# Moving the last two sums of W2's Strassen blocks to other places in VectorE's queue

## The chip, the cores and the metric

The kernel runs on one core of a Trainium2 chip. The metric is device time in microseconds (us) of one execution. The engines are named as in the profile: PE is the tensor engine, PEld its weight loads, DVE is VectorE, ACT is ScalarE, POOL is GpSimd and SP is SyncE. In these traces each engine works through its own queue in order.

## The reference

The program is a linear attention followed by a two-layer network. Cut to what matters:

```python
q_s = softmax(q, axis=-1)                        # 8 batches, 8 heads, 576 rows, 64 columns
k_s = softmax(k, axis=2)
kv  = einsum('bhsd,bhse->bhde', k_s, v)
x   = einsum('bhsd,bhde->bhse', q_s, kv)         # regrouped to 4608 x 512
h   = x @ w_in                                   # 512 x 2048
g   = h * sigmoid(h)
out = g @ w_out                                  # 2048 x 512
```

## The kernel before

The 4608 rows go through in nine chunks of 512 (the first two are of 576 and 448). In chunk t (t from 2 on) the tensor engine interleaves two kinds of work: the 16 **up-projections** of chunk t (`mm1`, numbered 0 to 15 in the order in which they run) and the output product of chunk t-1. That output product is done by Strassen's scheme of seven **products** in the order 1, 5, 6, 2, 7, 4, 3, each in two halves. Most of their operands are sums of blocks: `s_op` makes S1 to S4 from the activations in every chunk, and `t_op` makes T1 to T4 from W2 once in the program. Product 7 reads T3, and product 4 reads T4. All of these sums run on VectorE.

```python
def silu(t, fb, i, o, w):
    ...
    nc.scalar.activation(out=s, in_=i, func=ACT.Tanh, scale=OS)               # L244
    nc.vector.scalar_tensor_tensor(                                           # L245: "GT"
        out=o, in0=s, scalar=1.0, in1=i, op0=ALU.add, op1=ALU.mult)           # in1 is in PSUM

def mm1(t, fb):                      # one up-projection
    bank = hb[0] % hb[1]             # 3 banks from chunk 2 on
    hb[0] += 1
    mm1_mm(t, fb, bank, range(NC))   # L272
    mm1_silu(t, fb, bank)

def t_op(i, eng, f0=0, f1=HF):       # L345; all operands in SBUF
    o, in0, in1 = {
        1: (T1, B12, B11),
        2: (T2, B22, T1),
        3: (T3, B22, B12),           # T3 is written over B12 itself
        4: (T4, B21, T2),
    }[i]
    f = slice(f0, f1)
    eng.tensor_tensor(out=o[:, f], in0=in0[:, f], in1=in1[:, f], op=ALU.subtract)
```

There are three banks, so up-projection k can start only when VectorE has written GT of up-projection k-3. A VectorE that falls behind therefore stops the tensor engine three up-projections later.

The program is a list of units, one per up-projection or half product. `plan(u, f)` emits work just before unit u. In chunk 2, up-projections 0 to 12 are at units 0, 1, 3, 5, 7, 9, 11, 13, 15, 17, 19, 21 and 22. After the first product of the chunk (unit 2), units 21 and 22 are the only place where two come without a product between them. Product 7 begins at unit 18 and product 4 at unit 23. The units touched in chunk 2 (`begin[2]`):

```python
# sums of the activations, for every chunk t
plan(begin[t] + 2, lambda t=t: (s_op(t - 1, 1)))
plan(begin[t] + 4, lambda t=t: (s_op(t - 1, 2)))
plan(begin[t] + 10, lambda t=t: (s_op(t - 1, 3)))
plan(begin[t] + 15, lambda t=t: (s_op(t - 1, 4)))
# ... cut ...
plan(begin[2] + 7, lambda: t_op(4, nc.vector, 0, 4))
plan(begin[2] + 8, lambda: t_op(4, nc.vector, 4, 8))
plan(begin[2] + 12, lambda: t_op(3, nc.vector, 0, 4))
plan(begin[2] + 13, lambda: t_op(3, nc.vector, 4, 8))
# ... cut: the attention of the next batch b = t + 1, in each chunk t (units 5, 7 and 9, 12) ...
for i, x in enumerate((4, 6)):
    pl(x, lambda i=i, b=b: exp_q(b, i))
    pl(x + 1, lambda i=i, b=b: (qsum(b, i), qnorm(b, i, nc.gpsimd)))   # L142, L146 on VectorE; L151 on GpSimd
for i, x in enumerate((9, 12)):
    pl(x, lambda i=i, b=b: (exp_k(b, i), vcast(b, i, nc.gpsimd)))      # L89 on GpSimd
# (the loads of batch b + 1, which stand in these loops too, are cut)
```

The two `qnorm` instructions are called the norms below, and the two `vcast` instructions the casts.

The softmax here doesn't subtract the row's maximum and nothing guards it: scores larger than these inputs give would overflow.

Of the kernel before, what the change touches and what calls it, by code (L numbers as in the profile page):

```python
# [17 lines left out]
def kernel(  # L18
# [9 lines left out]
    nc = tc.nc  # L28
# [280 lines left out]
    def mm2_plain_out(t, ms):  # L309
        ow = mp.tile([128, 2, DM], FP32, name="ow", bufs=3)  # L310
        for i, m in enumerate(ms):
            if i == 0:
                nc.scalar.activation(out=ow[:, i], in_=PS[:, 2 + m], func=ACT.Copy, scale=OS)
            else:
                nc.vector.tensor_scalar_mul(out=ow[:, i], in0=PS[:, 2 + m], scalar1=OS)
            store(t, m * 128, ow[:, i])
# [20 lines left out]
    def t_op(i, eng, f0=0, f1=HF):  # L337
# [3 lines that stand above are left out]
            3: (T3, B22, B12),  # L341
# [4 lines that stand above are left out]
# [160 lines left out]
    def plan(u, f):  # L506
        at.setdefault(u, []).append(f)
# [7 lines left out]
    begin = {1: len(units)}  # L515
# [141 lines left out]
    for i, x in enumerate((25, 28)):  # L657
        plan(b1 + x, lambda i=i: xt(2, i))
    plan(b1 + 30, lambda: mm2_plain_out(0, (2, 3)))
    plan(begin[2] + 7, lambda: t_op(4, nc.vector, 0, 4))  # L660
    plan(begin[2] + 8, lambda: t_op(4, nc.vector, 4, 8))
    plan(begin[2] + 12, lambda: t_op(3, nc.vector, 0, 4))
    plan(begin[2] + 13, lambda: t_op(3, nc.vector, 4, 8))

    for t in range(2, NCH - 1):
        b = t + 1
# [58 lines left out]
```

## Time and profile before

| | before |
|---|---|
| median of the first three runs | 277.86 us (277.34 to 278.49) |
| the profiled execution | 277.1 us, span 275.3 us |
| chunk 2, first product to first product of chunk 3 | 31.04 us |
| chunk 3, measured likewise | 27.78 us |

The page's busy table says for each engine the busy time, the share of the span and the number of instructions:

```profile
PE 266.0 (97%) x2372; PEld 168.3 (61%) x2372; DVE 201.5 (73%) x291; ACT 158.3 (57%) x237; POOL 70.6 (26%) x62
```

The tensor engine bounds the kernel. The table of the tensor engine's waits says who waited for whom, the total in us, how often, and the longest:

```profile
PE PS L272 <- DVE GT L245: 2.4, 3, 1.2
```

Three waits, all in chunk 2, come to 2.4 us. The loss itself is better read from the tensor engine's timeline. Its columns are start, duration, engine and line, operation, operands, count, and in brackets the idle time before it and what ended it:

```profile
65.30 1.04 PE L361 MATMUL PS<-W,GT 128*128 128x256 f16 x8
...
76.22 1.02 PE L272 MATMUL PS<-XT,W 128*128 128x512 bf16 x4 [1.20 <-DVE GT L245]
...
79.08 1.02 PE L272 MATMUL PS<-XT,W 128*128 128x512 bf16 x4 [0.97 <-DVE GT L245]
...
81.17 1.02 PE L272 MATMUL PS<-XT,W 128*128 128x512 bf16 x4 [0.19 <-DVE GT L245]
82.14 1.19 PE L361 MATMUL PS<-W,S 128*128 128x256 f16 x8
83.33 1.02 PE L272 MATMUL PS<-XT,W 128*128 128x512 bf16 x4
...
96.34 1.04 PE L361 MATMUL PS<-W,GT 128*128 128x256 f16 x8
...
109.37 1.03 PE L272 MATMUL PS<-XT,W 128*128 128x512 bf16 x4
...
111.11 1.03 PE L272 MATMUL PS<-XT,W 128*128 128x512 bf16 x4
...
124.12 1.04 PE L361 MATMUL PS<-W,GT 128*128 128x256 f16 x8
```

The lines at 65.30, 96.34 and 124.12 us are the first half products of chunks 2, 3 and 4. Chunk 2 takes 31.04 us and chunk 3, with the same matmuls, 27.78 us. So chunk 2 loses 3.26 us, not 2.4. The rest hides where no idle time is recorded. In the undisturbed flow the record of one group overlaps the next by 0.17 us (65.30 + 1.04 = 66.34, and the next group starts at 66.17), so each of the three waits is recorded about 0.16 us too short: 0.5 us in all. The other 0.42 us is at product 7 (82.14), which shows 1.19 us instead of 1.04: the up-projection at 83.33 starts 2.16 us after the one at 81.17, where the undisturbed step in chunk 3 is 1.74 us (109.37 to 111.11). The Trainium skill ("Perfetto Trace Analysis", section "Identifying the Most-Contended Engine") warns that matmul busy time is a poor measure of how close a kernel is to roofline (its peak rate), because matmuls are pipelined. This trace agrees in so far as 0.9 of the 3.26 us does not appear as idle time.

Two timelines point to the cause. This is VectorE's, in chunk 2:

```profile
71.17 0.63 DVE L245 SCALAR_TENSOR_TENSOR GT<-sg,PS 128x512 f16<-128x512 f32 x1
71.71 2.35 DVE L345 TENSOR_TENSOR T<-W,T 128x1024 f16<-128x1024 f16 x1
73.98 1.34 DVE L142 TENSOR_REDUCE zq<-eq 128x18 f32<-128x1152 bf16 x1
...
75.54 0.63 DVE L245 SCALAR_TENSOR_TENSOR GT<-sg,PS 128x512 f16<-128x512 f32 x1
76.08 2.35 DVE L345 TENSOR_TENSOR T<-W,T 128x1024 f16<-128x1024 f16 x1
78.36 0.68 DVE L245 SCALAR_TENSOR_TENSOR GT<-sg,PS 128x512 f16<-128x512 f32 x1
78.95 1.56 DVE L335 TENSOR_TENSOR S<-GT 128x2048 f16<-128x2048 f16 x1
...
81.04 1.64 DVE L345 TENSOR_TENSOR W<-W 128x1024 f16<-128x1024 f16 x2
```

And this is GpSimd's:

```profile
71.40 2.12 POOL L151 TENSOR_TENSOR eq<-eq,rzq 128x1152 bf16<-128x1152 bf16 x1 [16.21 <-ACT sg L244]
75.77 2.12 POOL L151 TENSOR_TENSOR eq<-eq,rzq 128x1152 bf16<-128x1152 bf16 x1 [2.25 <-DVE rzq L146]
77.83 3.71 POOL L89 CAST vaug<-vt 128x1152 bf16<-128x1152 f32 x2
```

The two instructions of 2.35 us are T4's halves. Each starts 0.3 us after a norm and ends 0.54 us after the norm's end (73.52 and 74.06 for the first). The GT lines at 75.54 and 78.36 us end just when the tensor engine's waits end.

### The profile page before, as it was taken

To read this page: it belongs to the slowest core of one execution; us is meant where nothing else is said; L and a number is where in the kernel's file an instruction comes from. 1 tells how busy PE (TensorE), PEld (TensorE's weight loads), DVE (VectorE), ACT (ScalarE), POOL (GpSimd) and SP (SyncE) were. 2 spreads that over 40 slices of the span, in tenths; PEclk is the share of its full clock that TensorE was granted. 3 is DMA by queue.
4 is the path that set the end of the run, shared out by engine and by line. 5 is a ranking of instruction groups with operands and counts; after the bars stand their busy time and mean duration, and the time that the engine had idled before them with its cause. 6 is when DMAs were issued, how large, how long until landed. Compare 5 with 4: busy or idle time off the path is not lost.

```text
span 275.3 us, 5801 instructions
## 1 busy us (share of the span) xinstructions
PE 266.0 (97%) x2372; PEld 168.3 (61%) x2372; DVE 201.5 (73%) x291; ACT 158.3 (57%) x237; POOL 70.6 (26%) x62
## 2 busy tenths in 40 slices
PE   8999999999879999999999999999999999999993
PEld 3467654455645666656665666566656665666783
DVE  2867765969999399839984898489847673767643
ACT  5757937677833685467646764576455446444410
POOL 1744960900380019000900090009000000000003
PEclk9999999999999999999999999999999999999998
DMA  7999999599856386837693769342224003300444
GB/s 255 313 203 358 259 334 332 158 307 374 279 98 250 79 214 187 278 80 195 198 288 79 207 177 288 68 93 44 45 55 101 2 0 76 79 0 0 93 101 114
DMA packets 35498, 45.85 MB, mean 167 GB/s; under 512 B 16208, under 2 KB 20048, under 8 KB 35472
## 3 DMA queue, kind: packets, MB, share of 16 engines
q1 hardware_dynamic: 29568, 33.69, 43.6%
q0 software_dynamic: 5584, 11.54, 16.1%
q8 instruction: 18, 0.29, 0.5%
q10 hardware_dynamic: 320, 0.26, 0.3%
q14 instruction: 8, 0.07, 0.1%
HBM read 36.70 MB, written 9.44 MB: 168 GB/s over the span
## 4 chain that ended last, share of the span: by engine, by line
PE 85%; DVE 9%; ACT 2%; DMA 1%; POOL 1%; issue 1%; POOLq 0%
PE PS L272 38%; PE PS L361 34%; PE PS L301 5%; PE PS L252 4%; PE PS L222 2%; PE PS L183 2%; DVE zq L142 2%; DVE T L345 2%; DVE GT L245 2%; DVE S L335 1%; DMA qt<-in_q_dram 1%; DVE eq L151 1%; ACT eq L106 1%; ACT sg L244 1%; POOL t L120 0%
## 5 line engine op out<-in xcount | busy, mean ns | idle before, releaser
L245 DVE SCALAR_TENSOR_TENSOR GT<-sg,PS 128x512 f16<-128x512 f32 (+2 forms) x144 | 96.3, 678 | 53.3 <-ACT sg L244 52.9
L244 ACT ACTIVATE sg<-PS 128x512 f32<-128x512 f32 (+2 forms) x144 | 85.7, 598 | 83.7 <-PE PS L272 79.1
L272 PE MATMUL PS<-XT,W 128*128 128x512 bf16 (+1 forms) x512 | 126.5, 376 | 2.6 <-DVE GT L245 2.4
L272 PEld LDWEIGHTS <-W 128*128 128x128 bf16 x512 | 49.8, 98 | 42.0 <-issue 4.6
L361 PEld LDWEIGHTS <-S 128*128 128x128 f16 x512 | 49.1, 98 | 16.9 <-issue 1.4
L151 POOL TENSOR_TENSOR eq<-eq,rzq 128x1152 bf16<-128x1152 bf16 x13 | 27.5, 2117 | 107.8 <-ACT sg L244 98.2
L361 PEld LDWEIGHTS <-GT 128*128 128x128 f16 x384 | 37.1, 98 | 13.1 <-issue 1.2
L361 PE MATMUL PS<-W,S 128*128 128x256 f16 x256 | 33.1, 273 | 0.0
L361 PE MATMUL PS<-T,S 128*128 128x256 f16 x256 | 32.7, 273 | 0.0
L361 PE MATMUL PS<-W,GT 128*128 128x256 f16 x256 | 32.7, 273 | 0.0
L335 DVE TENSOR_TENSOR S<-GT 128x2048 f16<-128x2048 f16 (+1 forms) x17 | 24.3, 1427 | 0.0
L585 POOL DMA_DIRECT2D out_dram<-ow x4 | 2.2, 550 | 75.7 <-DVE ow L570 75.7
L106 ACT ACTIVATE eq<-qt 128x1152 bf16<-128x1152 f32 x16 | 18.6, 1164 | 2.5 <-DMA qt<-in_q_dram 2.5
L89 POOL CAST vaug<-vt 128x1152 bf16<-128x1152 f32 x12 | 19.9, 1686 | 0.0
L109 ACT ACTIVATE ek<-kt 128x1152 bf16<-128x1152 f32 x16 | 18.6, 1165 | 1.3 <-DMA kt<-in_k_dram 1.3
L87 ACT CAST XT<-PS 128x1024 bf16<-128x1024 f32 (+2 forms) x18 | 17.3, 961 | 2.9 <-PE PS L222 2.9
L142 DVE TENSOR_REDUCE zq<-eq 128x18 f32<-128x1152 bf16 x12 | 16.1, 1344 | 3.8 <-ACT eq L106 3.8
L252 PE MATMUL PS<-XT,W 128*128 128x288 bf16 x128 | 16.5, 286 | 0.7 <-DVE GT L245 0.4
L361 PE MATMUL PS<-T,GT 128*128 128x256 f16 x128 | 16.5, 273 | 0.0
L301 PE MATMUL PS<-W,GT 128*128 128x512 f16 x64 | 15.7, 380 | 0.0
L252 PEld LDWEIGHTS <-W 128*128 128x128 bf16 x128 | 12.4, 98 | 4.7 <-issue 1.7
L335 DVE TENSOR_TENSOR S<-GT,S 128x2048 f16<-128x2048 f16 x8 | 13.1, 1641 | 0.0
(58 smaller groups left out, 159.0 us busy)
## 6 DMA issues: line engine op xcount, KB each, us to landing
out_dram<-ow SPq DMA_DIRECT2D x64, 128.0 KB, 2.4
qt<-in_q_dram SPq DMA_DIRECT2D x12, 576.0 KB, 5.1
kt<-in_k_dram SPq DMA_DIRECT2D x12, 576.0 KB, 6.3
vt<-in_v_dram SPq DMA_DIRECT2D x12, 576.0 KB, 7.2
qt<-in_q_dram POOLq DMA_DIRECT2D x4, 576.0 KB, 13.6
kt<-in_k_dram POOLq DMA_DIRECT2D x4, 576.0 KB, 13.8
vt<-in_v_dram POOLq DMA_DIRECT2D x4, 576.0 KB, 13.7
W<-in_moe_w_out_dram POOLq DMA_DIRECT2D x4, 512.0 KB, 15.8
```

What stands on the lines that cost most here:

```text
L89: eng.tensor_copy(o, i)
L106: nc.scalar.activation(out=half(st[b]["eq"], cc), in_=jgd(b, "qt", cc), func=ACT.Exp)
L109: nc.scalar.activation(out=half(ek, cc), in_=jgd(b, "kt", cc), func=ACT.Exp)
L142: nc.vector.reduce_sum(out=z, in_=e, axis=AX.X)
L151: eng.tensor_tensor(out=e, in0=e, in1=r[:, :, :, None].to_broadcast([128, J, 2, D]), op=ALU.mult)
L244: nc.scalar.activation(out=s, in_=i, func=ACT.Tanh, scale=OS)
L245: nc.vector.scalar_tensor_tensor(out=o, in0=s, scalar=1.0, in1=i, op0=ALU.add, op1=ALU.mult)
L252: nc.tensor.matmul(out=PS[:, 2 * (fb % 3) + n, 0:S // 2], lhsT=W1[:, c, fb * 128:(fb + 1) * 128], rhs=XTS[0][:, c, n * (S // 2):(n + 1) * ...
L272: nc.tensor.matmul(out=PS[:, bank, o0:TCH], lhsT=W1[:, c, fb * 128:(fb + 1) * 128], rhs=XTS[t % 2][:, c, o0:TCH], start=(c == 0), stop=(c ...
L301: nc.tensor.matmul(out=PS[:, 2 + tb, :], lhsT=GTS[t % 2][:, fc, tb * 128:(tb + 1) * 128], rhs=W2[:, fc, :], start=(fc == 0), stop=(fc == N ...
L335: nc.vector.tensor_tensor(out=SS[i - 1][:, f], in0=in0[:, f], in1=in1[:, f], op=op)
L361: nc.tensor.matmul(out=PS[:, bank, m * HN:(m + 1) * HN], lhsT=a[:, fc, m * 128:(m + 1) * 128], rhs=bb[:, fc, :], start=(first and fc == 0) ...
```

## The change

The intent is to take T4's halves out from between the norms. T3 is also joined into one instruction, and goes in front of T4.

```diff
-    plan(begin[2] + 7, lambda: t_op(4, nc.vector, 0, 4))
-    plan(begin[2] + 8, lambda: t_op(4, nc.vector, 4, 8))
-    plan(begin[2] + 12, lambda: t_op(3, nc.vector, 0, 4))
-    plan(begin[2] + 13, lambda: t_op(3, nc.vector, 4, 8))
+    plan(begin[2] + 12, lambda: t_op(3, nc.vector))
+    plan(begin[2] + 14, lambda: t_op(4, nc.vector, 0, 4))
+    plan(begin[2] + 16, lambda: t_op(4, nc.vector, 4, 8))
```

## The prediction

> **What bounds it.** The tensor engine: 97% busy in the busy table, with the chain of waits 85% on it. The waits table gives it only 2.4 us of idle on VectorE's GT writes (the SiLU products), 2.2 us of that between 70 and 80 us, in chunk 2. The hidden loss is larger. In the timeline, chunk 2's first product starts at 65.30 us and chunk 3's at 96.34: 31.04 us. Chunk 3's stretch, with the same matmuls and no tensor-engine idle, takes 27.78 us (96.34 to 124.12). So chunk 2 loses about 3.26 us, through three stages: 1.37 us at up-projection 7, 2.49 by 8, 2.84 by 9, 3.26 by 10; nothing more after. The chain between 66 and 81 us runs on VectorE.
>
> **Why.** In the timeline each half of T4 takes 2.35 us on VectorE; the halves of T1 took 0.68 us. Each starts 0.3 us after a GpSimd norm (71.40 and 75.77 us, 2.12 us each) and ends 0.54 us after that norm. The Trainium skill, "SBUF — State Buffer", section "Who interferes with whom", says a VectorE instruction with two SBUF inputs contends with a GpSimd instruction that reads SBUF, and that the second waits for the first to end. This trace agrees: 2.35 = 1.8 waiting + 0.54 of work. The SiLU products (one input in PSUM) and the reductions do not stretch beside the norms.
>
> **The change.** It removes no arithmetic and one instruction (T3 undivided, about 0.07 us less). The two T4 halves (4.5 us of VectorE's line in chunk 2) leave the stretch between the norms; about 1.3 us of work comes back at units 14 and 16. Up-projections 7, 8 and 9 then have their banks in time. But now VectorE reaches S3 earlier, as in chunk 3, where S3 met the second norm and took 2.29 us (1.22 alone), and T3 and T4's first half meet the GpSimd casts (about 1.1 us each alone).
>
> My estimate, by shifting chunk 3's timeline by 31.04 us and inserting the three sums: S3 ends 76.8; T3 waits for the first cast, ends 78.9 (product 7 needs it at 79.2); GT 7 ends 79.5 (needed 80.1); T4 first half waits for the second cast, ends 80.5; S4 81.7; GT 8 82.3 (needed 82.6); T4 second half 82.9 (product 4 needs it after 84); then the `sa` addition, and GT 9 at 84.1, where up-projection 12 wants its bank at 83.5. So one stall of about 0.6 us remains: two up-projections without a product between them come just after the VectorE backlog. Gain: 3.26 - 0.6, about 2.7 us, all on the critical path, and kept to the end, since the tensor engine waits for nothing after chunk 2.
>
> **Prediction: 275.2 us (0.99 of before); 8 in 10: 274.4 to 276.2. Faster by over 2%: 0.01; within 2%: 0.98; slower: 0.01.**
>
> **What would show it.** The T4 halves near 1.1 and 0.7 us; the norms unchanged at 2.12 us, now back to back; S3 stretched from 1.56 to about 2.3 us; T3 about 1.6 us; the first product of chunk 3 about 2.7 us earlier; tensor-engine idle in chunk 2 down from 2.4 us to under 0.8 us, the remainder at the paired up-projections 11 and 12 and not at 7 and 8. Chunks 3 on unchanged but for the shift.
>
> **What would make it wrong.** If the second cast beats the waiting T3, T3 ends near 80 us and product 7 waits 0.8 us. If the backlog is smaller than I sum, the gain is the whole 3.2 us. If earlier stalls were hiding other late data (the transposed queries, the loads for batch 4), a new wait appears in chunk 2 or 3.

## The result and the profile after

| | before | after |
|---|---|---|
| median, first comparison (4 runs each) | 277.70 us | 274.36 us |
| ratio, 95% interval | | 0.9878 (0.9855 to 0.9902) |
| the profiled execution | 277.1 us | 274.3 us |
| span of the profile | 275.3 us | 272.5 us |
| chunk 2 | 31.04 us | 28.19 us |

Ratios here and below are the mean time of one kernel's runs over that of the other's in the same rounds, so they are not quite the ratio of the medians quoted. The change is within 2% and clearly a gain. The median lies 0.04 us under the predicted range.

The busy table after:

```profile
PE 263.6 (97%) x2343; PEld 168.4 (62%) x2372; DVE 199.2 (73%) x290; ACT 158.2 (58%) x237; POOL 71.1 (26%) x62
```

This trace lacks 29 matmul records (2343 against 2372 weight loads), so PE's busy sum is not compared. In the table of waits, what VectorE's GT costs the interleaved chunks is now:

```profile
PE PS L272 <- DVE GT L245: 0.3, 1, 0.3
```

The tensor engine's timeline after:

```profile
65.46 1.04 PE L361 MATMUL PS<-W,GT 128*128 128x256 f16 x8
...
75.01 1.03 PE L272 MATMUL PS<-XT,W 128*128 128x512 bf16 x4
...
82.80 1.03 PE L272 MATMUL PS<-XT,W 128*128 128x512 bf16 x3
84.08 1.02 PE L272 MATMUL PS<-XT,W 128*128 128x512 bf16 x4 [0.26 <-DVE GT L245]
...
93.65 1.04 PE L361 MATMUL PS<-W,GT 128*128 128x256 f16 x8
```

Up-projection 7 (75.01) no longer waits. One wait is left, at 84.08: up-projection 12, the second of the pair. Chunk 2 takes 93.65 - 65.46 = 28.19 us, which is 0.41 us more than chunk 3's 27.78 us. VectorE's timeline after, from the second reduction:

```profile
71.87 1.34 DVE L142 TENSOR_REDUCE zq<-eq 128x18 f32<-128x1152 bf16 x1
...
73.42 1.22 DVE L245 SCALAR_TENSOR_TENSOR GT<-sg,PS 128x512 f16<-128x512 f32 x2
74.56 2.29 DVE L335 TENSOR_TENSOR S<-GT 128x2048 f16<-128x2048 f16 x1
76.77 0.67 DVE L245 SCALAR_TENSOR_TENSOR GT<-sg,PS 128x512 f16<-128x512 f32 x1
77.37 1.57 DVE L345 TENSOR_TENSOR W<-W 128x2048 f16<-128x2048 f16 x1
78.86 0.68 DVE L245 SCALAR_TENSOR_TENSOR GT<-sg,PS 128x512 f16<-128x512 f32 x1
79.46 1.04 DVE L345 TENSOR_TENSOR T<-W,T 128x1024 f16<-128x1024 f16 x1
80.43 1.21 DVE L335 TENSOR_TENSOR S<-GT,S 128x2048 f16<-128x2048 f16 x1
81.56 0.67 DVE L245 SCALAR_TENSOR_TENSOR GT<-sg,PS 128x512 f16<-128x512 f32 x1
82.16 0.68 DVE L345 TENSOR_TENSOR T<-W,T 128x1024 f16<-128x1024 f16 x1
...
83.36 1.26 DVE L245 SCALAR_TENSOR_TENSOR GT<-sg,PS 128x512 f16<-128x512 f32 x2
```

And GpSimd's, where the norms now follow one another, as they do in chunk 3:

```profile
71.55 4.22 POOL L151 TENSOR_TENSOR eq<-eq,rzq 128x1152 bf16<-128x1152 bf16 x2 [16.21 <-ACT sg L244]
75.71 4.25 POOL L89 CAST vaug<-vt 128x1152 bf16<-128x1152 f32 x2
```

T4's halves fell from 2.35 us each to 1.04 and 0.68 us. In return S3 (74.56) now waits for the second norm: 2.29 us instead of 1.56. T3 and T4's first half meet the casts. The reduction at 71.87 us, with one input, lies wholly beside the first norm and takes its usual 1.34 us. The queue that this leaves ends with the GT at 83.36, which is the one up-projection 12 waits for.

The profiles account for the difference in time as follows. The start of chunk 2 is 0.16 us later after the change, chunk 2 is 2.85 us shorter, and from chunk 3 to the end it is 178.85 us against 178.96. That makes 2.8 us. But the medians of the first comparison lie 3.34 us apart. The experiments had to find where that 0.5 us is.

### The profile page after: what moved, and what is told of

It is laid out like the page before. It is cut to its first block, busy times and chain, and to the rows that moved or that the text cites. A ratio compares the mean times of both kernels' runs of the same rounds, so it can differ in the third digit from the quotient of the medians.

```text
span 272.5 us, 5771 instructions
## 1 busy us (share of the span) xinstructions
PE 263.6 (97%) x2343; PEld 168.4 (62%) x2372; DVE 199.2 (73%) x290; ACT 158.2 (58%) x237; POOL 71.1 (26%) x62
## 4 chain that ended last, share of the span: by engine, by line
PE 83%; DVE 8%; DMA 4%; ACT 2%; issue 1%; SPq 1%; POOL 1%; POOLq 0%
PE PS L272 36%; PE PS L361 33%; PE PS L301 5%; PE PS L252 4%; DMA vt<-in_v_dram 4%; DVE GT L245 2%; DVE S L335 2%; PE PS L222 2%; PE PS L183 2%; DVE zq L142 1%; SPq L95 1%; ACT sg L244 1%; DVE T L345 1%; DVE W L345 1%; POOL t L120 0%
## 5 line engine op out<-in xcount | busy, mean ns | idle before, releaser
L272 PE MATMUL PS<-XT,W 128*128 128x512 bf16 (+1 forms) x484 | 123.9, 375 | 1.8 <-DVE GT L245 0.3
L335 DVE TENSOR_TENSOR S<-GT 128x2048 f16<-128x2048 f16 (+1 forms) x17 | 25.0, 1470 | 0.0
```

The costliest lines, as they stand in the source:

```text
L272: nc.tensor.matmul(out=PS[:, bank, o0:TCH], lhsT=W1[:, c, fb * 128:(fb + 1) * 128], rhs=XTS[t % 2][:, c, o0:TCH], start=(c == 0), stop=(c ...
L335: nc.vector.tensor_tensor(out=SS[i - 1][:, f], in0=in0[:, f], in1=in1[:, f], op=op)
```

## The experiments

**Theory.** The norms' reads of SBUF held T4 up; the gain is the 3.26 us lost in chunk 2 less a rest of 0.4 us; the first timings of before sat high. **Rivals.** (1) The gain is really 3.3 us, with a part that the profile of before did not have. (2) T4 was simply too much work for VectorE at that place, whatever GpSimd did. (3) A part of the gain comes from joining T3.

The table gathers what the profiles of all runs say. "Chunk 2" runs from its first product to that of chunk 3, and "rest" from there to the end of the span. Spans are given to 0.1 us.

| run | chunk 2 starts | chunk 2 | rest | median us | ratio to before, 95% |
|---|---|---|---|---|---|
| before, first profile | 65.30 | 31.04 | 179.0 | 277.70 | |
| before_again | 65.90 | 31.04 | 179.1 | 277.08 | 0.9998 (0.9985 to 1.0011) |
| before_third | 65.07 | 31.05 | 179.1 | 277.17 | 0.9995 (0.9977 to 1.0012) |
| after, first profile | 65.46 | 28.19 | 178.9 | 274.36 | 0.9878 (0.9855 to 0.9902) |
| after_again | 65.50 | 28.20 | 179.0 | 274.49 | 0.9903 (0.9889 to 0.9918) |
| after_third | 65.33 | 28.19 | 179.1 | 274.33 | 0.9892 (0.9875 to 0.9909) |
| t4_moved_only | 65.78 | 28.86 | 179.1 | 274.89 | 0.9913 (0.9898 to 0.9928) |
| t3_whole_only | 65.32 | 31.27 | 179.0 | 277.41 | 1.0010 (0.9997 to 1.0022) |
| norm_writes_only | 65.09 | 27.78 | 179.0 | 273.91 | 0.9877 (0.9861 to 0.9893) |
| t4_before_norms | 65.78 | 28.58 | 178.9 | 274.77 | 0.9905 (0.9891 to 0.9920) |
| t4_in_chunk1 | 66.05 | 27.78 | 178.9 | 274.36 | 0.9888 (0.9872 to 0.9905) |
| t4_second_at_18 | 65.82 | 27.78 | 178.9 | 274.11 | 0.9878 (0.9864 to 0.9893) |
| t4_at_18_again | 65.24 | 27.78 | 179.1 | 273.86 | 0.9876 (0.9858 to 0.9895) |

Runs of one call shared a chip and the runs of before. The first call held after_again, before_again, t4_moved_only and t3_whole_only. The second held norm_writes_only and the three that place T4 elsewhere. The third held after_third, t4_at_18_again and before_third.

### The two kernels once more (after_again, before_again)

Neither has an edit.

> The changed kernel once more, unaltered, to size the gain. The two profiles show the span 2.8 us shorter (275.3 to 272.5), chunk 2 2.85 us shorter (31.04 to 28.19, first product to first product of the next chunk), yet the medians differ by 3.3 us. Theory A (the profile is the truth; three timings of before sat high): ratio about 0.9899 (2.8 us of 277.1). Theory B (the gain is really 3.3 us, and the profiled execution of before was a quick one): ratio about 0.988.

> The kernel before, unaltered, as a null: ratio 1.000 within 0.2%. What it tells: the spread of the times and a second profile. Theory A: times mostly near 277.1 to 277.5 and chunk 2 again 31.04 us. Theory B: times 277.3 to 278.5, and a profile whose excess over 275.3 us lies in some stretch that can be named; if the collisions with the norms fall differently from one execution to the next, the excess lies in chunk 2; if it is start-up loading, it lies before 65 us.

The medians were 274.49 and 277.08 us, against 277.19 us over nine timings of before; the ratios were 0.9903 and 0.9998. Theory A fits and theory B's 0.988 lies below the interval. Chunk 2 of before took 31.04 us in both profiles, so the collisions with the norms do not fall differently from one execution to the next. The second profile's span is 0.7 us longer (276.0 us), and 0.6 of that is before chunk 2: it starts at 65.90 us instead of 65.30. Start-up is what varies in the profiles. This one can be traced further: the tensor engine is still level when chunk 0's up-projections begin (15.40 and 15.39 us), and 0.62 us behind at the next group (27.85 and 28.47). In between, the second profile's weight loads wait twice for the DMA of `w_in`, 0.7 us in all; the first profile has no such wait.

### Only T4 moved (t4_moved_only)

```diff
-    plan(begin[2] + 7, lambda: t_op(4, nc.vector, 0, 4))
-    plan(begin[2] + 8, lambda: t_op(4, nc.vector, 4, 8))
     plan(begin[2] + 12, lambda: t_op(3, nc.vector, 0, 4))
     plan(begin[2] + 13, lambda: t_op(3, nc.vector, 4, 8))
+    plan(begin[2] + 14, lambda: t_op(4, nc.vector, 0, 4))
+    plan(begin[2] + 16, lambda: t_op(4, nc.vector, 4, 8))
```

> Only T4's halves move to units 14 and 16; T3 stays in two halves at 12 and 13. If leaving the norms is all of the gain: as the changed kernel within 0.1 us plus 0.07 us for one more instruction. Rival: joining T3 matters[...]: then T3's second half ends about 1.1 us later (near 80.0 us), product 7 and up-projection 10 wait about 0.8 us, and the time is about 0.8 us above the changed kernel.

VectorE's timeline of this run:

```profile
77.70 2.59 DVE L345 TENSOR_TENSOR W<-W 128x1024 f16<-128x1024 f16 x2
80.22 0.67 DVE L245 SCALAR_TENSOR_TENSOR GT<-sg,PS 128x512 f16<-128x512 f32 x1
```

And GpSimd's:

```profile
76.04 3.71 POOL L89 CAST vaug<-vt 128x1152 bf16<-128x1152 f32 x2
```

T3 in two halves takes 2.59 us where T3 whole took 1.57 us: 1.02 us more, as the rival said. The two casts took 2.15 and 1.62 us, where the shortest cast of the kernel before took 1.16. So the second, recorded from 78.1 us, was held up by T3's first half (until 78.73) and then ran to 79.75. T3's second half, 1.63 us by itself, ended at 80.29, 0.54 us after that cast, just as T4's halves ended 0.54 us after the norms. The cast had gone between the halves. Chunk 2 is 0.67 us longer than in the changed kernel (28.86 against 28.19), and the median is 0.40 us higher. So leaving the norms is most of the gain (31.04 to 28.86 us), and joining T3 adds 0.67 us to it. The expected sizes, 1.1 us for T3 and 0.8 us for the time, were a little large.

### Only T3 joined (t3_whole_only)

```diff
-    plan(begin[2] + 12, lambda: t_op(3, nc.vector, 0, 4))
-    plan(begin[2] + 13, lambda: t_op(3, nc.vector, 4, 8))
+    plan(begin[2] + 12, lambda: t_op(3, nc.vector))
```

> Only T3 joined at unit 12; T4's halves stay at 7 and 8 beside the norms. If leaving the norms is all of the gain: ratio 1.000 (at most 0.1 us less), T4's halves 2.35 us each, chunk 2 about 31.0 us. Rival (joining T3 carries part of the gain): 0.3 us or more less.

The ratio is 1.001 and T4's halves keep their 2.35 us, so joined T3 gains nothing by itself. It even makes chunk 2 0.23 us longer (31.27 us). The tensor engine's timeline shows why, at product 7:

```profile
82.69 1.05 PE L361 MATMUL PS<-W,S 128*128 128x256 f16 x8 [0.48 <-DVE W L345]
```

With T3 in halves, product 7 began at 82.14 us, while VectorE was still at T3; joined, the product waits for all of it. The same edit costs 0.23 us beside T4 at its old place and saves 0.67 us beside T4 at its new one, because only there does a cast stand waiting between the halves.

### Norms that write and do not read (norm_writes_only)

The base is the kernel with only T3 joined, so T4 stays at units 7 and 8. Batch 3's two norms, which are the ones in chunk 2, become fills. The values are wrong. (The comparison with the reference still passed; the rows of `eq` are softmaxes of small numbers, so 1/64 everywhere is probably close to them.)

```diff
+    def fake_norm(b, cc):
+        for _ in range(2):
+            nc.gpsimd.memset(half(st[b]["eq"], cc), 1.0 / D)
...
-    pl(x + 1, lambda i=i, b=b: (qsum(b, i), qnorm(b, i, nc.gpsimd)))
+    pl(x + 1, lambda i=i, b=b: (qsum(b, i), fake_norm(b, i) if b == 3 else qnorm(b, i, nc.gpsimd)))
```

> Wrong outputs on purpose. T4's halves stay at units 7 and 8 (T3 joined, as in the run with T3 alone joined), but batch 3's two GpSimd norms are replaced by two GpSimd fills each of the same tile, which write it and read nothing. If the norms' reads hold T4 up: T4's halves fall from 2.35 to about 0.7 us each beside busy GpSimd, the tensor engine has no wait in chunk 2, chunk 2 falls from 31.27 us to about 27.8 us. Rival (T4 in that place is simply too much VectorE work before up-projections 7 to 9, or any GpSimd instruction holds it up): the waits of 1.2 and 0.96 us largely stay, chunk 2 above 30 us.

VectorE's timeline (the added lines move L345 to L349):

```profile
71.51 0.68 DVE L349 TENSOR_TENSOR T<-W,T 128x1024 f16<-128x1024 f16 x1
...
74.21 0.68 DVE L349 TENSOR_TENSOR T<-W,T 128x1024 f16<-128x1024 f16 x1
```

And GpSimd's:

```profile
70.81 2.17 POOL L157 MEMSET eq<- 128x1152 bf16 x2 [15.83 <-DVE zq L142]
73.50 2.17 POOL L157 MEMSET eq<- 128x1152 bf16 x2 [0.53 <-DVE zq L142]
```

GpSimd is busy for 2.17 us around each half of T4, as long as a norm, and each half takes 0.68 us. Chunk 2 falls from 31.27 to 27.78 us, exactly chunk 3's time, with T4 at its old units. So the place is not too early by itself and rival 2 falls. What cost the time was a VectorE sum with two SBUF inputs beside a GpSimd instruction that reads SBUF. (A fill differs from a norm in more than reading: it does another operation, and two of them fill the time of one norm. The casts, which read too, hold such sums up as the norms do.) The Trainium skill ("SBUF — State Buffer", section "Who interferes with whom") says the same: such a sum contends with a GpSimd instruction that reads SBUF, and not with one that only writes it. Here that is 2.35 us beside the norms and 0.68 us beside the fills.

### T4's second half later still (t4_second_at_18, t4_at_18_again)

```diff
-    plan(begin[2] + 16, lambda: t_op(4, nc.vector, 4, 8))
+    plan(begin[2] + 18, lambda: t_op(4, nc.vector, 4, 8))
```

> The changed kernel with T4's second half at unit 18 instead of 16, behind the SiLU product that up-projection 12 waits for. If the remaining loss of 0.41 us in chunk 2 is the queue in front of that product: it goes, chunk 2 falls from 28.19 to about 27.8 us, the ratio to before about 0.9888 (0.4 us under the changed kernel). Rival (it only moves to the next up-projection, or product 4 waits for T4): chunk 2 stays at 28.1 to 28.3 us.

The tensor engine's timeline shows the pair of up-projections 11 and 12 as one run, without a wait:

```profile
83.17 1.89 PE L272 MATMUL PS<-XT,W 128*128 128x512 bf16 x8
```

VectorE's shows T4's second half behind the GT that up-projection 12 needs:

```profile
83.12 0.67 DVE L245 SCALAR_TENSOR_TENSOR GT<-sg,PS 128x512 f16<-128x512 f32 x1
83.72 0.68 DVE L345 TENSOR_TENSOR T<-W,T 128x1024 f16<-128x1024 f16 x1
```

Chunk 2 takes 27.78 us, so the whole loss is gone. This shows that the rest of 0.41 us was the VectorE queue in front of this GT. The changed kernel was not in this call, so the version was run once more beside it.

> Chunk 2 again 27.78 us, so 0.41 us shorter than the changed kernel's; the median 0.3 to 0.5 us below the changed kernel's of the same call. Rival: the start-up's spread of some tenths of a microsecond hides it, and the medians do not differ.

> The changed kernel beside the version with T4's second half at unit 18, on one chip. Chunk 2 again 28.2 us. The median again 274.4 to 274.6 and before again near 277.2: then the three first timings of before, with their median of 277.86, sat high by about 0.6 us. Rival: before near 277.8 again, so the times of before drift from chip to chip and the gain with them (ratio near 0.988).

> A third profile of the kernel before: chunk 2 again 31.04 us to within 0.05; the start of chunk 2 anywhere between 65.0 and 66.0 us, so that the spread from one execution to another lies in start-up and not in the collisions with the norms. Rival: chunk 2 is the part that varies.

The medians were 273.86 us against 274.33 us for the changed kernel, a difference of 0.47 us for the 0.41 us of chunk 2. Before's chunk 2 was 31.05 us again. The three profiles of before put the start of chunk 2 at 65.07, 65.30 and 65.90 us. 27 timings of the kernel before have a median of 277.20 us (276.78 to 278.08). This version beats the kernel before clearly. Against the changed kernel, chunk 2 is 0.41 us shorter in both of its profiles and the median agrees, but the ranges of the timings overlap (273.65 to 274.62 against 274.14 to 274.63), so the times alone do not settle it.

### T4 in chunk 1's tail (t4_in_chunk1)

```diff
-    plan(begin[2] + 14, lambda: t_op(4, nc.vector, 0, 4))
-    plan(begin[2] + 16, lambda: t_op(4, nc.vector, 4, 8))
+    plan(b1 + 26, lambda: t_op(4, nc.vector, 0, 4))
+    plan(b1 + 29, lambda: t_op(4, nc.vector, 4, 8))
```

> The changed kernel with both T4 halves in chunk 1's tail (units 26 and 29 of chunk 1), where VectorE has idle time and GpSimd does nothing. If VectorE's gaps there are truly free: chunk 2 about 27.8 us, the start of chunk 2 not later, the ratio about 0.9888. Rival: the tail of chunk 1 has one up-projection after another, so VectorE's delays of 0.6 us hold up its banks and the gain of 0.4 us is given back before chunk 2 begins (its start 0.2 to 0.4 us later).

Chunk 2 takes 27.78 us, as hoped. But the stretch of chunk 1 from the matmuls after `kv_both` (40.38 us in the profile after, 40.44 us here) to the start of chunk 2 takes 25.61 us against 25.08 us. VectorE's gaps of up to 0.7 us there were not free: one up-projection follows another, and the tensor engine's timeline has a new wait:

```profile
64.06 2.15 PE L272 MATMUL PS<-XT,W 128*128 128x512 bf16 x8 [0.22 <-DVE GT L245]
```

The 0.53 us lost in chunk 1 undo the 0.41 us won in chunk 2. The median, 274.36 us, is the changed kernel's. The rival had it right, and the loss was above its 0.2 to 0.4 us.

### T4 in front of the norms (t4_before_norms)

```diff
-    plan(begin[2] + 14, lambda: t_op(4, nc.vector, 0, 4))
-    plan(begin[2] + 16, lambda: t_op(4, nc.vector, 4, 8))
+    plan(begin[2] + 5, lambda: t_op(4, nc.vector))
```

> The changed kernel with T4 whole at unit 5 of chunk 2, in front of the first reduction: clear of the norms on their early side. T4 takes 1.22 us. If clear of the norms is all that matters: as the changed kernel or better. My sum, with the VectorE queue followed instruction by instruction: the norms and all that follows start about 1.1 us later, up-projection 7 waits 0.2 us, product 7 waits about 0.6 us for T3; chunk 2 about 28.6 us, so 0.4 us slower than the changed kernel and still 2.4 us faster than before.

Chunk 2 took 28.58 us, against 28.6 expected. T4 took 1.22 us, undisturbed. But T3 came late for product 7:

```profile
80.46 1.05 PE L361 MATMUL PS<-W,S 128*128 128x256 f16 x8 [0.40 <-DVE W L345]
```

So being clear of the norms is not all that matters. The work also has to stand behind whatever the tensor engine needs next.

## Why the prediction was right or wrong

- **The mechanism was right.** The norms held T4 up, and moving T4 away freed the tensor engine. The waits at up-projections 7, 8 and 9 went, and the norms kept 2.1 us each and followed one another. T4's halves took 1.04 and 0.68 us (forecast 1.1 and 0.7), S3 2.29 (2.3) and T3 1.57 (1.6). The one wait left was at up-projection 12. The fills show the cause: norms that write and do not read cost nothing. One value was missed: the prediction booked joining T3 as 0.07 us less work, but with T3 left in halves chunk 2 is 0.67 us longer (28.86 us). The sum for the change as made does not rest on this, because it took T3 whole.
- **The cost of chunk 2 was right.** The estimate of 3.26 us is confirmed by the two correct versions that remove it all (t4_in_chunk1 and t4_second_at_18): they reach 27.78 us, 3.26 under 31.04.
- **The rest was sized a little high.** The prediction put it at 0.6 us; it measured 0.41 us. Set 0.16 us back for the later start of chunk 2, the measured ends lie before the forecast ones by 0.11 us at S3 (76.69 for 76.8), 0.16 at T4's first half (80.34 for 80.5) and 0.22 at S4 (81.48 for 81.7), and by about as much at every later step, GT 9 included. So these three sums were each taken a little long, and GT 9 came about 0.2 us earlier than summed. The gain in chunk 2 was 2.85 us, not 2.7.
- **The failed step is the base from which the gain was subtracted: 277.86 us.** The prediction does not name its base, but 277.86 - 2.7 = 275.16: it took the median of three timings and wrote 275.2. The profile that all its readings came from was of an execution of 277.1 us, and 27 later timings have a median of 277.20 us. The base was 0.66 us too high. With it and the 0.15 us above, 275.2 - 0.66 - 0.15 = 274.39 us; measured were 274.36, 274.49 and 274.33. The range of 274.4 to 276.2 was laid around the same base; 0.66 us lower it would have held the measured time. That the miss was of only 0.04 us is no merit of the sum: the two errors, 0.66 and 0.15 us, point the same way.
- **What stays open.** The profiles of before differ by up to 0.8 us in when chunk 2 starts, by under 0.02 us in chunk 2, and by about 0.1 us after it. So start-up varies, and that is shown. The slowest execution of before that was profiled (277.79 us) lost its 0.6 us to late loads of `w_in`. No profile exists of one of the executions of 278 us (three of the 27 timings are above 277.8), so it is not shown that the first three timings sat high for that reason. Rival 1, that the gain is really 3.3 us, has little left: three profiles of each kernel agree on chunk 2 to 0.01 us and on the rest to 0.2 us, and the repeats gave 0.9903 (its interval just excludes 0.988) and 0.9892 (its interval still includes it).

## What to carry to other kernels

Subtract a predicted gain from the execution whose profile gave the gain, or from a median of many timings, and not from a median of three: here that choice was worth 0.66 us, more than all errors of the mechanism. Size a loss by comparing a stretch with a like one that is undisturbed (31.04 against 27.78 us), since recorded idle time showed only 2.4 of 3.26 us. When a sum on VectorE with two SBUF inputs must move, follow the whole queue behind it instruction by instruction, including which GpSimd instruction stands waiting and which result the tensor engine needs next.

## What the Trainium skill lacked or had wrong

- "SBUF — State Buffer", section "Who interferes with whom", says that issue order decides who blocks, but gives no example with both engines' queues full. Here, when the second norm ended, the sum that had been waiting went ahead of the cast queued behind the norm (S3, 2.29 us in the changed kernel; the cast took 2.15 us, where the shortest took 1.16). And when T3's first half ended, the waiting cast went ahead of T3's second half. So cutting a VectorE sum in two let a GpSimd instruction in: 2.59 us for two halves, 1.57 us for the whole.
- The same page does not say what a blocked sum costs beyond the wait. T4's half ended 0.54 us after the norm's end, while undisturbed it lasts 0.68 us as recorded, so no extra delay is seen here.
